# An attention and MLP kernel: key and value tokens laid out four and three to a partition, and a new order of the first batch's steps

## The chip, the core and the metric

The kernel runs on one core of a Trainium2 chip. Its metric is the device time of one execution in microseconds (us). The engines have names of two to four letters: PE multiplies matrices, DVE and ACT work on vectors, POOL is the general engine that also issues the loads which change their type, and SP issues all other loads and stores. Each engine has its own queue of instructions and takes them strictly in order; semaphores tie the queues together. SBUF is the on-chip memory of 128 partitions, PSUM the memory into which PE writes.

## What is computed

Eight batches of twelve heads, 448 tokens of 64 numbers each. Queries and keys are normalized by their root mean square and a gain, then comes softmax attention without a mask. The heads' results, side by side, are the rows of a 3584 x 768 matrix that goes through an MLP with 2048 hidden units and the tanh form of GELU.

```python
q_n, k_n = rmsnorm(q, g_q), rmsnorm(k, g_k)          # x / sqrt(mean(x*x) + 1e-6) * g
scores = scale * q_n @ k_n.T                         # per batch and head, scale = 1/8
attn = exp(scores - max) / sum(exp(scores - max))
x = (attn @ v).transpose(0, 2, 1, 3).reshape(3584, 768)
h = x @ w_in                                         # 768 -> 2048
out = gelu_tanh(h) @ w_out                           # 2048 -> 768
```

The order of a batch's keys within a head is free, as long as keys and values are laid out alike: attention sums over them.

## The kernel before

**Pairs and chunks.** The twelve heads of a batch are six pairs (`hp` 0 to 5), three chunks `c` of two pairs `j` = 0 and 1. For a chunk, `load_q` (L114) and `load_k` (L130) bring queries and keys into the tiles `rawq` and `rawk` (four buffers each). All these loads are issued by SP in the order of `loads` (L146): queries of pair 0, keys of pair 0, queries of pair 1, keys of pair 1, and two small ones.

**Where the keys lie.** 448 keys are three full tiles of 128 and a rest of 64. A key tile has seven slots per chunk (`NS` = 7): slots 0 to 2 hold the first 384 keys of pair 0, slots 4 to 6 those of pair 1, and slot 3 is shared: the last 64 keys of pair 0 lie in partitions 0 to 63, those of pair 1 in 64 to 127 (`own(j)`, L127). `main(j)` loads 384 keys over 128 partitions, three in a row to a partition; `last(j)` loads the other 64. Values follow the same places: `vb` holds three slots of each head, `vr` the rest, with zeros in the partitions of the other pair. `load_v` (L151) is issued by POOL, which turns float32 into bfloat16 on the way: part 0 loads `vb`, parts 1 and 2 load `vr`.

**From raw to exponentials.** Per chunk and pair: squares (`square`, L174), sums of squares on DVE (`total`, L202), one over the root by a logarithm and an exponential on ACT (`rsqrt`, L205), the product with it (`normed`, L219), transposes on PE (`trans`, L231), copies from PSUM into `qT` and `kT` on DVE or ACT (`place_q`, `place_k`). `scores` (L300) then computes one of seven tiles of a chunk ("r" is the shared slot) and returns its exponential, which runs on ACT. Two places in PSUM take scores (`spots`), a third after `third` (L294), and the MLP's first product (`mm1`, L399) uses the same places.

**Sums and products.** `pair_products` (L350) with `what` = 0 sums a pair's exponentials on PE, with `what` = 1 it multiplies them by the values. In the first batch both come in two halves (`sa`, `sb` and `xa`, `xb`). `recip_in`, `recip` and `recip_out` turn the sums into reciprocals on DVE by a transpose, a reciprocal and a transpose back, and `pair_x` multiplies.

**The order of the first batch.** In the first batch the order of all engines' work is written out by hand, in the string `FRONT` (L761), whose steps `front` (L669) issues one by one; each engine gets its instructions in that order. A letter behind the colon says on which engine a step runs (A for ACT, D for DVE, P for POOL). The names:

- `sq`, `sk`: squares of queries or keys of pair i; `tq`, `tk`: their sums; `nq`, `nk`: norms; `tpq`, `tpk`: transposes; `cq`, `ck`: copies out of PSUM
- `rs` i: the roots of pair i; `rS` c: the roots of both pairs of chunk c
- `s` n, `e` n: scores and exponential of tile n, 0 to 20, seven per chunk; `st`, `rc`, `rb`, `xt`: the steps behind a pair's sums
- `v` i, `w` i, `o` i: loads of values, of a quarter of `w_in`, of a quarter of `w_out`, all on POOL; `L` bc: the loads of batch b, chunk c, on SP
- `y` n: n products of zeros on PE, 224 columns each (`idle`, L214), whose result nobody reads
- `gcol`, `shift`: the gains and a bound for the exponent; `mb`, `ma`, `mc`, `md`: parts of the MLP's first product, `g` its GELU; capital letters (`Sq`, `Tk`, `Rs`, `Nk`, `Tp`, `Cq`): the second batch's squares, sums, roots and so on; `V` its values; `GELU`, `EXP`: loads of ACT's function table

**Later batches.** From the second batch on, `attention` (L513) weaves a batch's scores and products with the MLP's second product (`mm2`, L431) of the batch before, so that PE always has something to do; loads come one or two batches ahead, and keys and queries are transposed by DMA (`dma_trans`, L266).

## Time and profile before

| | us |
|---|---|
| median of 3 runs (lowest, highest) | 413.26 (412.65, 413.44) |
| the profiled execution, its own time | 413.83 |
| the profiled execution, its span | 412.1 |

| engine | busy us | share of the span |
|---|---|---|
| PE | 403.7 | 98% |
| ACT | 296.2 | 72% |
| DVE | 274.3 | 67% |
| POOL | 131.8 | 32% |

The span runs from the first to the last instruction of the program. All times inside it count from its start. A row of the list in order of time gives start, duration, engine, line of the kernel, operation, what is written and read, their shapes, and in brackets how long the engine had been idle and what ended that. An engine with a q behind its name (SPq) is its sequencer, which issues DMAs. The granted clock is the share of its full clock at which PE was allowed to run. The trace lacks a few per cent of the products, so counts of them are a little low.

### The profile page before, as it was taken

To read this page: it belongs to the slowest core of one execution; us is meant where nothing else is said; L and a number is where in the kernel's file an instruction comes from. 1 tells how busy PE (TensorE), PEld (TensorE's weight loads), DVE (VectorE), ACT (ScalarE), POOL (GpSimd) and SP (SyncE) were. 2 spreads that over 40 slices of the span, in tenths; PEclk is the share of its full clock that TensorE was granted. 3 is DMA by queue.
4 is the path that set the end of the run, shared out by engine and by line. 5 is a ranking of instruction groups with operands and counts; after the bars stand their busy time and mean duration, and the time that the engine had idled before them with its cause. 6 is when DMAs were issued, how large, how long until landed. Compare 5 with 4: busy or idle time off the path is not lost.

```text
span 412.1 us, 10085 instructions
## 1 busy us (share of the span) xinstructions
PE 403.7 (98%) x4207; PEld 243.5 (59%) x4207; DVE 274.3 (67%) x454; ACT 296.2 (72%) x398; POOL 131.8 (32%) x144
## 2 busy tenths in 40 slices
PE   8799999999999999999999999999999999999996
PEld 3344555566655666557655666556655575556664
DVE  4899739899899638884678747786488633783010
ACT  5797987969988587767977778785976558774300
POOL 7689000234500942037500745019310460000000
PEclk9699999999999999999999999999999999999999
DMA  8999995999981689229981399616991161210022
GB/s 191 227 235 228 203 196 141 227 227 192 213 145 38 139 176 207 66 52 176 222 140 41 78 203 171 136 40 145 171 145 40 23 112 40 72 46 2 2 77 78
DMA packets 97870, 54.21 MB, mean 132 GB/s; under 512 B 63776, under 2 KB 94368, under 8 KB 97824
## 3 DMA queue, kind: packets, MB, share of 16 engines
q1 hardware_dynamic: 71392, 41.69, 43.4%
q0 software_dynamic: 26112, 11.80, 22.5%
q8 instruction: 33, 0.54, 0.6%
q10 hardware_dynamic: 320, 0.07, 0.1%
q14 instruction: 13, 0.11, 0.1%
HBM read 45.61 MB, written 11.01 MB: 137 GB/s over the span
## 4 chain that ended last, share of the span: by engine, by line
PE 95%; SPq 2%; DMA 1%; DVE 0%; ACT 0%; issue 0%; ACTq 0%; DVEq 0%
PE o L441 36%; PE hh L412 31%; PE o L370 11%; PE sc L324 8%; PE h L412 5%; PE sc L310 1%; DMA rawq<-in_q_dram 1%; PE ox L370 1%; SPq L143 1%; SPq L118 1%; SPq L136 1%; PE tp L245 0%; PE o L477 0%; PE tp L238 0%; ACT ex L331 0%
## 5 line engine op out<-in xcount | busy, mean ns | idle before, releaser
L441 PE MATMUL o<-wout,g 128*64 128x384 bf16 (+1 forms) x1648 | 160.6, 327 | 0.0
L331 ACT ACTIVATE ex<-sc,shift 128x896 bf16<-128x896 f32 x144 | 136.1, 1011 | 1.3 <-PE sc L324 1.3
L412 PE MATMUL hh<-xT,win 128*64 128x448 bf16 (+1 forms) x1260 | 133.8, 353 | 0.0
L441 PEld LDWEIGHTS <-g 128*64 128x64 bf16 (+1 forms) x1648 | 96.2, 109 | 58.3 <-issue 14.8
L412 PEld LDWEIGHTS <-win 128*64 128x64 bf16 (+1 forms) x1440 | 95.4, 109 | 49.9 <-issue 3.2
L421 ACT ACTIVATE g<-hh 128x896 bf16<-128x896 f32 x56 | 50.1, 919 | 44.5 <-PE hh L412 44.4
L203 DVE TENSOR_REDUCE ss<-sq 128x14 f32<-128x896 f32 (+4 forms) x45 | 47.9, 1080 | 32.4 <-ACT sq L186 19.9
L454 ACT COPY osb<-o 128x384 f32<-128x384 f32 x50 | 24.2, 483 | 47.8 <-PE o L441 47.8
L788 POOL COPY mark<-es 1x1 bf16<-1x1 bf16 x8 | 1.8, 225 | 162.9 <-DVE es L345 158.5
L377 DVE STREAM_TRANSPOSE st<-o 128x448 f32<-128x448 f32 x48 | 31.1, 648 | 23.6 <-PE o L370 23.2
L324 PE MATMUL sc<-qT,kT 64*128 64x448 bf16 (+1 forms) x372 | 39.6, 360 | 1.7 <-DVE kT L264 1.3
L345 DVE TENSOR_TENSOR es<-ex 128x896 bf16<-128x896 bf16 x42 | 26.8, 637 | 12.0 <-ACT ex L331 12.0
L226 POOL TENSOR_TENSOR nrmq<-rawq,rinv 112x512 bf16<-112x512 f32 x33 | 34.0, 1043 | 0.0
L226 POOL TENSOR_TENSOR nrmk<-rawk,rinv 128x512 bf16<-128x512 f32 (+1 forms) x33 | 31.1, 957 | 4.2 <-ACT rinv L212 4.2
L385 DVE STREAM_TRANSPOSE rb<-rc 128x448 f32<-128x448 f32 x48 | 31.0, 645 | 1.6
L370 PE MATMUL o<-ex,vb 128*64 128x448 bf16 x252 | 30.9, 352 | 0.0
L279 DVE TENSOR_SCALAR kT<-kT,gcol 128x896 bf16<-128x896 bf16 x19 | 21.1, 1108 | 11.7 <-DMA kT<-nrmk 11.7
L343 DVE TENSOR_TENSOR es<-es,exr 64x896 bf16<-64x896 bf16 x42 | 25.9, 617 | 2.4 <-ACT exr L331 1.0
L345 DVE TENSOR_TENSOR es<-es,ex 128x896 bf16<-128x896 bf16 x42 | 25.5, 608 | 2.3 <-ACT ex L331 0.3
L395 DVE TENSOR_TENSOR xT<-o,rb 128x448 bf16<-128x448 f32 x42 | 25.8, 615 | 1.4 <-PE o L370 0.9
L188 POOL TENSOR_TENSOR sq<-rawq 112x1024 f32<-112x1024 f32 x9 | 17.0, 1893 | 28.4 <-DMA rawq<-in_q_dram 25.0
L324 PEld LDWEIGHTS <-kT 64*128 64x128 bf16 (+1 forms) x372 | 10.9, 99 | 24.6 <-issue 18.1
(83 smaller groups left out, 349.4 us busy)
## 6 DMA issues: line engine op xcount, KB each, us to landing
rawq<-in_q_dram SPq DMA_DIRECT2D x48, 224.0 KB, 4.4
rawk<-in_k_dram SPq DMA_DIRECT2D x48, 192.0 KB, 4.6
vb<-in_v_dram POOLq DMA_DIRECT2D x8, 576.0 KB, 10.1
win<-in_moe_w_in_dram POOLq DMA_DIRECT2D x4, 768.0 KB, 14.1
wout<-in_moe_w_out_dram POOLq DMA_DIRECT2D x4, 768.0 KB, 20.4
out_dram<-osb SPq DMA_DIRECT2D x7, 336.0 KB, 4.3
out_dram<-osb SPq DMA_DIRECT2D x8, 288.0 KB, 2.7
out_dram<-osb SPq DMA_DIRECT2D x8, 240.0 KB, 2.6
```

Source lines behind the costliest of these rows:

```text
L203: nc.vector.reduce_sum(stat(ssq[b % 3], b, c, n, j), view(n, sqs[n, b, c], j), axis=AX.X)
L226: eng.tensor_mul(dst.rearrange("p t a d -> p a t d"), view(n, raws[n, b, c], j), r.to_broadcast(list(r.shape) + [D]),)
L324: nc.tensor.matmul(sc[o, a, :S], kT[r, c, 4 * j + t, o], qT[b][r, hp], start=True, stop=True,)
L331: nc.scalar.activation(dst, sc[:, :, :S], AF.Exp, scale=scale, bias=shift)
L343: nc.vector.tensor_add(es[p], es[p], exrs[b, hp // 2][p])
L345: nc.vector.tensor_add(es, ex[:, 0] if t == 1 else es, ex[:, t])
L370: nc.tensor.matmul(o[a * D:(a + 1) * D], w(a), e[:, a], start=(i == 0), stop=(i + 1 == len(steps)),)
L377: nc.vector.transpose(oas["st"].rearrange("p a b -> p (a b)"), oas[0])
L385: nc.vector.transpose(oas["rb", hp], oas["rc"].to_broadcast([128, S // 32, 32]))
L412: nc.tensor.matmul(h[i * m:(i + 1) * m, j, :S], win[:, c // 2 + NCH * (c % 2), f * 128 + i * m:f * 128 + (i + 1) * m], xT[b][:, c], start= ...
L421: nc.scalar.activation(g[:, fs[0]:fs[0] + len(fs), (b % 2) * S:(b % 2 + 1) * S], hs1[fs[0]][:, :, :S], AF.Gelu_apprx_tanh)
L441: nc.tensor.matmul(o[j * m:(j + 1) * m, :HD], g[:, f, i * 128 + j * m:i * 128 + (j + 1) * m], wout[:, f, half * HD:(half + 1) * HD], start ...
```

## The change

Three things change together.

- **Layout of keys and values.** The first 256 keys of a head now lie four in a row in the 64 partitions of `own(j)`, the other 192 three in a row in the other 64 partitions. Both parts of a pair's keys are loads over 64 partitions (`part`), in the order queries, keys, keys per pair. The slots of `rawk` and `kT` are used as before, the shared slot included. Values get a fourth slot in `vb`, and `vr` goes; what was zero in `vr` is zero in `vb`. A batch's values are four loads, two in part 0 and one each in parts 1 and 2.
- **Products with the values.** The same eight products per pair, in the same order; the ones with the shared slot now read `vb`.
- **Order of the first batch.** `FRONT` is a new string: the second chunk's roots are one step (`rS1`), some squares and norms run on another engine, values are loaded in another order, `w0` to `w3` are issued later, zero products stand in other places (`y` 4, 4, 2, 1, 1, 1 instead of 3). The loads of the second batch's first chunk are the first step of `FRONT` instead of standing in front of it. A step `H` is defined, which the string does not use.

```diff
-    vb = [wts.tile([128, H, NK, D], BF16, name=f"vb{i}") for i in range(2)]
-    vr = [wts.tile([128, 2, HP, D], BF16, name=f"vr{i}") for i in range(2)]
+
+    vb = [wts.tile([128, H, NK + 1, D], BF16, name=f"vb{i}") for i in range(2)]
...
-    SM = 128 * NK
+    SM = 64 * (NK + 1)
+
+    def keys(j, n):
+        return (own(j), slice(0, SM)) if n > NK else (own(1 - j), slice(SM, S))
...
-        def main(j):
+        def part(j, n):
+
+            at, span = keys(j, n)
+            s = slice(NK * j + j * (n == NK), NK * j + j * (n == NK) + n)
             h = head(c, j)
             nc.sync.dma_start(
-                t[:, :, 4 * j:4 * j + NK],
-                k[b, h:h + 2, :SM].rearrange("a (p t) d -> p a t d", t=NK),
+                t[at, :, s], k[b, h:h + 2, span].rearrange("a (p t) d -> p a t d", t=n)
             )
-
-        def last(j):
-            h = head(c, j)
-            nc.sync.dma_start(t[own(j), :, NK], k[b, h:h + 2, SM:].rearrange("a p d -> p a d"))
-        return [lambda: main(0), lambda: main(1), lambda: last(0), lambda: last(1)]
+        return [lambda j=j, n=n: part(j, n) for j in range(2) for n in (4, 3)]
 
     def loads(b, c):
         lq, lk = load_q(b, c), load_k(b, c)
-        for go in (lq[0], lk[0], lq[1], *lk[1:]):
+        for go in (lq[0], *lk[:2], lq[1], *lk[2:]):
             go()
 
     def load_v(b, part):
-        if part == 0:
+
+        for j, n in ((0, NK), (1, NK)) if part == 0 else ((part - 1, NK + 1),):
+            at, span = keys(j, n)
+            first = j * (n == NK)
             nc.gpsimd.dma_start(
-                vb[b % 2].rearrange("p h t d -> p h (t d)"),
-                v[b, :, :SM].rearrange("h (p t) d -> p h (t d)", t=NK),
-            )
-        else:
-            j = part - 1
-            nc.gpsimd.dma_start(
-                vr[b % 2][own(j), j], v[b, HP * j:HP * j + HP, SM:].rearrange("h p d -> p h d")
+                vb[b % 2][at, HP * j:HP * j + HP, first:first + n].rearrange("p h t d -> p h (t d)"),
+                v[b, HP * j:HP * j + HP, span].rearrange("h (p t) d -> p h (t d)", t=n),
             )
...
         if what:
-            steps = [(main[t], lambda a, t=t: vb[b % 2][:, head(c, j) + a, t]) for t in range(NK)]
-            steps.append((exrs[b, c], lambda a: vr[b % 2][:, j, 2 * c + a]))
+            steps = [
+                (e, lambda a, t=t: vb[b % 2][:, head(c, j) + a, t])
+                for t, e in enumerate(main[:NK * (1 - j)] + [exrs[b, c]] + main[:NK * j])
+            ]
+            if j:
+                steps.append(steps.pop(0))
...
     loads(0, 2)
-    loads(1, 0)
...
     for i in range(2):
-        nc.gpsimd.memset(vr[i], 0.0)
+        for j in range(2):
+            nc.gpsimd.memset(vb[i][own(1 - j), HP * j:HP * j + HP, NK * (1 - j)], 0.0)
...
     FRONT = """
-        sq0:A sk0:P gcol tq0 tk0 sq1:P rs0 sk1:A nq0:P v1 nk0:D shift tq1 tk1 sq2:A tpq0 tpk0 v2
-        v0 sk2:A rs1 sq3:A cq0:D ck0:D tq2 s0 e0 y3 s1 nk1:D nq1:D L11 e1 tpk1 tpq1 s2 sk3:P w0
-        tq3 tk2 rs2 e2 ck1:D cq1:D s3 e3 sa0 s4 sk4:P tk3 nq2:D nk2:D rs3 tpk2 tpq2 s5 sb0 tk4
-        ck2:D cq2:D nq3:D st0 e4 nk3:P e5 s6 sk5:P L12 e6 tpk3 tpq3 s7 e7 s8 sa1 s9 sb1 xa0 e8
-        sq4:P sq5:P w1 rc0 cq3:D rb0 ck3:D tq4 tk5 rs4 e9 xb0 s10 st1 xt0 rc1 rb1 tq5 e10 sa2
-        s11 e11 rs5 nk4:P nq4:P w2 nk5:P nq5:P xa1 xb1 sb2 s12 e12 s13 tpk4 tpq4 xt1 st2 ck4:D
-        cq4:D rc2 xa2 e13 rb2 sa3 xb2 s14 tpk5 tpq5 s15 e14 xt2 ck5:D cq5:D sb3 e15 U s16 s17
-        xa3 xb3 s18 w3 o0 Sk0:P e16 st3 rc3 rb3 e17 xt3 e18 s19 sa4 xa4 sb4 xb4 Tk0 st4 rc4 s20
-        mb0 mb1 mb2 mb3 sa5 e19 e20 o1 Sq0:P Sq1:P V0 rb4 GELU xt4 Tq0 xa5 sb5 xb5 st5 V1 V2 o2
-        o3 Sk1:A rc5 rb5 ma1 mc0 mc1 xt5 md0 ma2 md1 mc2 md2 Tq1 Tk1 g0 EXP md3 Rs0 g1 Nk00:D
-        Nq11:D Nq00:D Tp0 md4 Cq0:A g2 Sq2:A g3 Nk10:D Nk01:D Nq01:D Ck0:D Tp1 md5 Sk2:A Tq2 Tk2
-        Nk11:D Nq10:D Ck1:A g4 Cq1:A g5 md6 md7 g6 g7 md8 g8
+        L10 sq0:A tq0 sk0:D tk0 gcol rs0 sk1:A sq1:P v1 nq0:P v2 nk0:D tq1 tk1 shift sq2:A rs1
+        tpk0 y4 tpq0 y4 v0 nq1:P sq3:A sk2:P ck0:D cq0:D s0 e0 s1 y2 nk1:D L11 e1 tpk1 s2 tpq1
+        sk3:P e2 ck1:D tq2 cq1:D s3 y1 sa0 s4 e3 s5 sb0 tk2 tq3 tk3 sk4:P rS1 e4 nk2:D nq2:D s6
+        tpk2 y1 tpq2 y1 tk4 st0 ck2:D cq2:D e5 sq4:A nk3:P nq3:P sq5:P w0 sk5:P L12 e6 tpk3 s7
+        sa1 e7 s8 tpq3 sb1 s9 xa0 rc0 tq4 rb0 ck3:D tq5 cq3:D st1 e8 rs4 e9 xb0 s10 xt0 tk5 rc1
+        e10 sa2 s11 xa1 sb2 xb1 s12 rs5 e11 e12 nk4:P nq4:P nq5:P nk5:P w1 w2 w3 Sk0:P rb1 st2
+        xt1 tpq4 tpk4 s13 xa2 e13 cq4:D ck4:D tpq5 s14 tpk5 xb2 s15 sa3 sb3 e14 cq5:D rc2 rb2
+        ck5:D xt2 e15 U s16 s17 s18 xa3 xb3 e16 st3 rc3 rb3 e17 xt3 o0 Sq0:P e18 sa4 s19 sb4 xa4
+        xb4 mb0 mb1 s20 st4 Tk0 rc4 mb2 mb3 Sq1:A e19 e20 rb4 xt4 Tq0 sa5 sb5 xa5 xb5 st5 o1
+        Sk2:P V0 V1 V2 Sk1:A GELU Sq2:A o2 rc5 rb5 mc0 ma1 mc1 xt5 md0 md1 ma2 mc2 md2 Tk1 Tq1
+        g0 EXP Rs0 g1 g2 md3 Nq00:D Nk00:D Tp0 md4 o3 g3 Ck0:A Nk10:D Nk11:D Nq01:D Nq11:D
+        Nk01:D Nq10:D Cq0:D md5 Tp1 g4 g5 Ck1:D Tq2 Cq1:D Tk2 md6 md7 g6 g7 md8 g8
 """
```

More of the change, by code (lines that the diff above doesn't have):

```diff
@@ L112, in head, with raw_q @@
         return 2 * c + HP * j
+    def raw_q(b, c):
+        if ("q", b, c) not in raws:
+            raws["q", b, c] = rawqk.tile([P, CH, NQ, D], F32, tag="rawq", name="rawq")
+        return raws["q", b, c]
     def load_q(b, c):
-        t = rawqk.tile([P, CH, NQ, D], F32, tag="rawq", name="rawq")
-        raws["q", b, c] = t
+        t = raw_q(b, c)
         return [
@@ L734, in front @@
             loads(*divmod(i, 10))
+        elif name == "H":
+            eng.memset(raw_q(*divmod(i, 10))[:1, 0, 0, :1], 0.0)
         elif name in ("Sq", "Sk"):
```

## The prediction

> **What bounds the kernel now.** I read the page first, then busy time by stretch, then the instructions in order of time up to the second batch.
>
> ```profile
> span 412.1 us, 10085 instructions
> PE 95%; SPq 2%; DMA 1%; DVE 0%; ACT 0%; issue 0%; ACTq 0%; DVEq 0%
> ```
>
> TensorE (PE) carries 95% of the chain that ended last, so time can only come from where it idles, repeats work or runs slowly. The second view finds those places. Its columns after the stretch are the length, then busy time and count on PE, weight loads, VectorE (DVE), ScalarE (ACT) and GpSimd (POOL), then the granted TensorE clock, DMA share and GB/s.
>
> ```profile
> 7.17:14.00 6.83, 4.34 (x34) 2.06 (x32) 6.11 (x13) 4.71 (x8) 6.06 (x7) 1.00 1.22 227
> 14.00:20.83 6.83, 6.05 (x37) 2.45 (x36) 5.57 (x13) 5.67 (x9) 4.03 (x5) 0.50 1.37 230
> 20.83:27.66 6.83, 6.42 (x63) 2.96 (x62) 6.72 (x15) 6.51 (x11) 5.45 (x6) 1.00 1.17 243
> 27.66:37.20 9.54, 9.54 (x85) 4.34 (x81) 8.80 (x16) 9.21 (x10) 9.51 (x9) 1.00 1.19 230
> 37.20:54.85 17.65, 17.65 (x105) 9.27 (x104) 11.28 (x17) 13.16 (x18) 3.67 (x5) 1.00 1.37 202
> 54.85:340.00 285.15, 285.15 (x3202) 177.04 (x3203) 208.19 (x330) 219.04 (x293) 98.46 (x101) 1.00 0.69 137
> ```
>
> From 54.85 us to 340 us PE never idles: whatever moves there moves nothing. The tail behind it isn't touched. What this change can win lies before 54.85 us: 2.49 us of idle PE in 7.17 to 14.00, and one stretch of 6.83 us at half clock. The start of the second batch's scores at 54.85 is therefore the mark; if they start x earlier, the kernel ends x earlier.
>
> The third view gives the rows of the first batch that set that mark (start, duration, engine, line).
>
> ```profile
> 11.13 1.91 ACT L331 ACTIVATE ex<-sc,shift 128x896 bf16<-128x896 f32 x2
> 14.39 0.31 ACT L209 ACTIVATE lg<-ss,eps 128x14 f32<-128x14 f32 x1 [1.36 <-DVE ss L203]
> 14.85 0.99 ACT L331 ACTIVATE ex<-sc,shift 128x896 bf16<-128x896 f32 x1
> 17.11 1.01 ACT L331 ACTIVATE ex<-sc,shift 128x896 bf16<-128x896 f32 x1
> 19.77 1.01 ACT L331 ACTIVATE ex<-sc,shift 128x896 bf16<-128x896 f32 x1 [0.37 <-PE sc L324]
> 21.09 1.90 ACT L331 ACTIVATE ex<-sc,shift 128x896 bf16<-128x896 f32 x2 [0.31 <-PE sc L324]
> 25.12 1.00 ACT L331 ACTIVATE ex<-sc,shift 128x896 bf16<-128x896 f32 x1
> 32.25 2.82 ACT L331 ACTIVATE ex<-sc,shift 128x896 bf16<-128x896 f32 x3
> 37.20 5.09 PE L412 MATMUL hh<-xT,win 128*128 128x448 bf16 x26
> 54.85 0.74 PE L324 MATMUL sc<-qT,kT 64*128 64x448 bf16 x6
> ```
>
> The 21 exponentials (e0 to e20) start at 11.13 and end at 32.25 + 2.82 = 35.07, 23.94 us for 21 pieces of some 0.94 (2.82 / 3), so 4.2 us are gaps and roots. The largest gap is the 1.36 us in front of the root at 14.39: it waits on DVE for a sum of squares, and e2 (14.85) is queued behind it on ACT although its scores are ready. After 37.20 PE runs through.
>
> **The change part by part.** All times below are on the clock of this execution.
>
> ```profile
> 1.19 0.46 SPq L136 DMA_DIRECT2D rawk<-in_k_dram  x1
> 2.75 1.41 SPq L143 DMA_DIRECT2D rawk<-in_k_dram  x2
> 6.13 1.04 POOL L188 TENSOR_TENSOR g<-rawq 112x512 f32<-112x512 f32 x1 [0.93 <-DMA rawq<-in_q_dram]
> 7.13 1.36 POOL L226 TENSOR_TENSOR nrmq<-rawq,rinv 112x512 bf16<-112x512 f32 x1
> 8.43 1.48 POOL L159 DMA_DIRECT2D vr<-in_v_dram  x2
> 8.78 1.27 DVE L203 TENSOR_REDUCE ss<-g 112x8 f32<-112x512 f32 x2
> 9.96 0.38 DVE L255 COPY qT<-tp 128x448 bf16<-128x448 bf16 x1
> 10.26 0.41 DVE L264 TENSOR_SCALAR kT<-tp,gcol 128x384 bf16<-128x384 bf16 x1
> 10.54 0.61 ACT L186 ACTIVATE g<-rawq 112x512 f32<-112x512 f32 x1
> 11.02 0.46 PE L217 MATMUL w<-zeros 128*128 128x224 bf16 x3
> 11.71 1.04 POOL L188 TENSOR_TENSOR g<-rawk 128x512 f32<-128x512 f32 x1 [0.76 <-DMA rawk<-in_k_dram]
> 11.78 1.53 DVE L226 TENSOR_TENSOR nrmq<-rawq,rinv 112x512 bf16<-112x512 f32 x1
> 12.71 0.89 POOL L630 DMA_DIRECT2D win<-in_moe_w_in_dram  x1
> 13.62 0.84 POOL L188 TENSOR_TENSOR g<-rawk 128x384 f32<-128x384 f32 x1
> 15.57 0.67 DVE L226 TENSOR_TENSOR nrmq<-rawq,rinv 112x512 bf16<-112x512 f32 x1
> 16.17 0.54 DVE L226 TENSOR_TENSOR nrmk<-rawk,rinv 128x384 bf16<-128x384 f32 x1
> ```
>
> *Loads of keys.* Two issues over 128 partitions (0.46 each) and two over 64 (1.41 / 2 = 0.70) become four over 64. A chunk costs SP 4 x 0.70 instead of 2 x 0.46 + 1.41: 0.47 more. No row shows 64 partitions with runs of 1024 or 768 bytes; its bounds are 0.46 and 0.70, and I take 0.70 as the nearer in partitions. It lies behind the transfers, which are saturated (DMA share 1.22 to 1.37 from 7.17 to 20.83), and the bytes of a chunk stay. With that cover gone the second half of a later chunk lands up to 0.5 later per chunk. In the other batches PE hides it whole. The Trainium skill, "DMA: Bandwidth & Descriptors", Rules for kernel authors, speaks against such a split: two transfers to disjoint partition halves serialize, and one over 128 partitions is to be used. By that rule the split earns nothing and its issue times come out as loss; what that makes here is rival 5.
>
> *Loads of v.* Three issues (two of 0.74, and one over 128 partitions) become four over 64, some 3.0 us of POOL. What counts is place: one issue now stands between POOL's square (6.13 to 7.17) and the norm nq0, which starts at 7.9 instead of 7.13; three more stand ahead of nq1, now on POOL. Queued behind them: nq1, then the squares sk2, sk3 and the root over both.
>
> *First pair.* The square sk0 moves from POOL to DVE; no row shows an f32 product of that form on DVE; its bounds are 0.54 (the norm at 16.17) and 0.84 (POOL at 13.62), I take 0.54. Behind the sum over q it ends no earlier than on POOL: nothing gained. nq0 ends at 7.9 + 1.04 = 8.95 (8.49 before). DVE reaches ck0 and cq0 after two sums (end 8.9) and three small steps of the shift (some 0.5): 9.4 + 0.41 + 0.38 = 10.2. Scores 0.36 later, 10.6; but ACT must first do sq3, whose load doesn't come earlier (it ran at 10.54 before; I take 10.2 + 0.61). So e0 at 10.85: 0.3 gained.
>
> *Roots of the second chunk at once.* e0 to e3 now follow each other: e3 ends at 10.85 + 4 x 0.94 = 14.6. e3 needs nq1: POOL 8.95 + 3 x 0.74 + 1.04 = 12.2, transposes and copy (0.38) and scores: 13.4, just in time. The one root over 30 columns needs both POOL squares: 12.2 + 0.84 + 1.04 = 14.1, a sum 0.64 (1.27 / 2), then 0.46 as between 14.39 and 14.85, and the steps from engine to engine: e4 at 15.35 instead of 17.11. Lead 1.75. One root fewer, 0.46, is in it.
>
> *The lead is spent.* sq4 moves to ACT: 0.61 ahead of e6, which still starts at 17.9 instead of 19.77. For e7, DVE does nk2 and nq2 from 15.35 (0.54 + 0.67) while POOL does nk3 and nq3. At 11.78 such a norm on DVE, beside the POOL square of 11.71, took 1.53 instead of 0.67; the bounds of that penalty are 0 and 0.86, and I take half. With a sum, a transpose and two copies (0.64 + 0.65 + 0.41 + 0.38: DVE done at 19.0) and scores e7 starts at 19.4 instead of 21.09: lead 1.7. Then DVE has reciprocal and transpose of pair 0 (38.64 - 36.93 - 0.65 = 1.06), three sums (1.92), a transpose, a product (0.62) and two copies (0.79), 5.0 together, before the root of the third chunk's second half: 18.7, from overlaps of some 0.06 a step, + 5.0 + 0.46 puts e11 at 24.2 instead of 25.12. From there the exponentials run on: e18 at 24.2 + 7 x 0.94 = 30.8 instead of 32.25. Sq1 of the second batch, now on ACT between e18 and e19, is twice the 0.61 of 10.54 at most; I take 1.1. e20 ends at 34.7: 0.4 gained.
>
> ```profile
> 35.63 1.21 DVE L203 TENSOR_REDUCE ss<-sq 112x16 f32<-112x1024 f32 x1
> 36.93 0.65 DVE L377 STREAM_TRANSPOSE st<-o 128x448 f32<-128x448 f32 x1
> 38.64 0.62 DVE L395 TENSOR_TENSOR xT<-ox,rb 128x448 bf16<-128x448 f32 x1
> 40.12 0.92 ACT L421 ACTIVATE g<-hh 128x896 bf16<-128x896 f32 x1 [2.78 <-PE hh L412]
> 45.25 2.43 PE L412 MATMUL hh<-xT,win 128*128 128x448 bf16 x12
> ```
>
> *The end of the first batch.* Only the last sums wait for e20. PE gets through them at some 36.0 instead of 37.20, and its twelve products before md0 (12 x 5.09 / 26 = 2.35) end at 38.35 instead of 39.55. md0 also needs the last product on DVE (38.64 + 0.62 = 39.26 before). Its chain, 2.33 from the transpose at 36.93 to that end, now stands behind the sum Tq0 (1.21, the form of 35.63): from 34.9 that ends at 36.1, and 36.1 + 2.33 = 38.4. So md0 at 38.5 to 38.6 instead of 39.55. The first gelu (40.12) follows it, then two table loads with the root between, the second gelu, and the products at 45.25 that wait for its place: 0.9 to 1.0 earlier, as the two sums that this root still needs (2 x 1.21) end on DVE at 40.8. The squares of the second batch that change engines lie behind PE's products.
>
> *Zero products.* Three go, thirteen come, each 0.46 / 3 = 0.15 alone: 1.5 us of PE, where it otherwise waits for norms; without that wait they would cost it.
>
> *Weights.* w0's issue moves from 12.71 behind the square sq5 (15.35 + 3 x 1.04 and half the penalty) to 19, and its products start behind e18. The view of this tile gives
>
> ```profile
> DMA to landing us min/median/max: 11.6/14.1/15.7
> ```
>
> from issue to landing, for parts that all had v or another part ahead on their queue; w0 now has nothing ahead. Bounds: 19 + 11.6 to 19 + 15.7, or earlier by the wait it no longer has. I take 29 and no cost; at 34.7 it would hold PE's first eight products by 2 us, which the last key sums could partly fill. The zeroing of v's unused places is as large as before, and POOL waits for data then.
>
> *Sum.* 0.3 at e0, 1.7 at e7, 0.4 at e20, but 0.9 at md0, since PE and DVE had less left behind the exponentials. So -0.9 +- 0.5 at 54.85, and at the end. This execution took 413.83 by its own time (span 412.1, 1.7 around it): 412.9. The median of three is 413.26, 0.57 less: **412.35**.
>
> **The clock.** This sum holds at full clock. The stretch from 7.17, PE busy 4.34 of 6.83 (64%), is followed by half clock; those with 6.05 (89%) and 6.42 (94%) by full. So the limit of what counts as busy lies between 64% and 89%. Changed, the first gains eight zero products net, a score and the first key sums, 1.2 to 2.2 us: 81 to 95%, probably enough. The next stretch, now at full speed, does the same work in less time; I put it at 65 to 85%. The Trainium skill, "TensorE: Matmul & The Clock Gate", Why this matters for your kernels, asks only that no gap exceeds about 3 us. By that rule neither kernel would lose its clock, and rivals 1 and 2 would have no chance; the trace disagrees: the stretch before the slow one has only 2.49 us of idle time in all.
>
> **The rivals.**
> 1. *The slow stretch moves to 20.83 to 27.66.* For: the 65 to 85% above. Against: it is only about half of the open interval. Price: before has 63 products there, 0.098 each (half of 5.09 / 26, as most use half of the array) and the transposes among them half of that, 4.5 to 5.5 us with what has been done earlier; at half clock 9 to 11, 2.2 to 4 more than the 6.83 hold. Less the lead of 0.9: +1.3 to +3; I take the lower end, as PE also has short waits there to fill, +1.2: 414.45, slower. It decides from the point where the loss exceeds 0.9.
> 2. *It stays at 14.00 to 20.83.* Transposes and scores on e7's path take 0.2 each longer, and the sums too: 0.5 lost, 412.85. For: ten small zero products are little work. Against: the 81 to 95%.
> 3. *The lead is eaten.* DVE and POOL get in each other's way at nk2/nq2 beside nk3/nq3 by the full 0.85, nq1 comes late for e3, and Sq1 (1.06) stands in front of e19: e20 no earlier, 413.3. For: the row at 11.78. Against: DVE and PE have less left behind e20.
> 4. *The lead lasts*, should the third chunk's root not hold e11: 1.7 as at e7, 411.55. Against: DVE is busy for 6.72 of 6.83 us from 20.83.
> 5. *The split loads cost their issue.* The queries of the second chunk come behind one chunk's 0.47 more on SP, sq3 and e0 with them: 412.35 + 0.5 = 412.85. Against: the DMA share above 1.2 says that data, not issue, is late.
>
> **How the numbers follow.** Forecast 0.52, rivals 0.18, 0.12, 0.10, 0.04 and 0.04. Beyond 0.2% (0.83 us, about what a measurement of this kernel tells from no change) lie 412.43 and 414.09. Faster: 0.36 of the forecast (its centre is just past the bound, and between bounds I mostly took the longer step), 0.02 of rivals 2 and 5, 0.04 of rival 4: 0.42. Slower: 0.16 of rival 1, 0.02 of rival 3, 0.01 of the forecast: 0.19. Same: 0.39. The range for 8 in 10 is 411.4 to 414.5: the top reaches rival 1's price, the bottom rival 4's. The forecast's own range is 411.85 to 412.85.
>
> **What would show it.** Right: e2 directly behind e1, one root before e4 at 15 to 15.6, e7 near 19.4, e20 ending near 34.7, md0 near 38.5, second batch's scores near 53.9, full clock throughout. Wrong: half clock at 14.00 or 20.83; a norm on POOL or DVE over 1.3 us; e3 waiting for nq1; any PE idle after the second batch's scores.

## The result and the profile after

| | before | after |
|---|---|---|
| median, us | 413.24 | 414.19 |
| lowest to highest of 22 runs | 412.11 to 414.29 | 413.36 to 416.59 |
| ratio after / before, 95% interval | | 1.0033 (1.002 to 1.0045) |
| profiled execution, its own time | 413.83 | 414.39 |
| its span | 412.1 | 412.6 |

The change makes the kernel 0.95 us slower; the forecast was 0.9 us faster. First the view of busy time by stretch, in the stretches and columns of the prediction, and the one row for all that follows the mark.

```profile
7.17:14.00 6.83, 5.21 (x42) 2.53 (x41) 6.27 (x14) 5.24 (x9) 6.81 (x9) 1.00 1.11 211
14.00:20.83 6.83, 4.50 (x34) 1.90 (x33) 5.47 (x12) 5.29 (x8) 4.88 (x6) 0.87 1.24 212
20.83:27.66 6.83, 6.83 (x59) 2.71 (x57) 5.40 (x12) 6.15 (x11) 5.30 (x6) 0.88 1.18 219
```

```profile
55.43:340.00 284.57, 284.57 (x3198) 177.00 (x3199) 209.15 (x330) 218.56 (x292) 101.13 (x107) 1.00 0.68 139
```

In 7.17 to 14.00 PE is busier (5.21 for 4.34), as forecast. In 14.00 to 20.83 it is busy for 4.50 where before had 6.05: new waits, though part of those 6.05 us is products that ran at half clock. A clock of 0.87 and 0.88 in two stretches is one piece of half clock that lies across 20.83. The same view in stretches of 3.41 us places it:

```profile
12.29:15.70 3.41, 2.83 (x23) 1.00 (x21) 2.89 (x6) 2.95 (x5) 2.11 (x3) 1.00 1.24 202
15.70:19.11 3.41, 1.25 (x15) 0.81 (x12) 2.56 (x6) 3.31 (x5) 2.77 (x3) 1.00 1.28 220
19.11:22.53 3.42, 3.36 (x20) 1.21 (x19) 2.88 (x8) 1.87 (x2) 3.40 (x4) 0.50 1.13 223
22.53:25.94 3.41, 3.41 (x34) 1.41 (x32) 2.52 (x6) 3.10 (x8) 1.90 (x4) 1.00 1.21 206
```

PE is busy for 1.25 of 3.41 us from 15.70, and half clock follows, 19.11 to 22.53. From there on PE has no idle time: what it loses at half clock in that stretch is not made up in this execution. What made the stretch from 15.70 so empty is in the list in order of time:

```profile
10.98 2.80 ACT L334 ACTIVATE ex<-sc,shift 128x896 bf16<-128x896 f32 x3
15.57 0.23 ACT L215 ACTIVATE rinv<-lg 128x30 f32<-128x30 f32 x1
15.70 1.89 ACT L334 ACTIVATE ex<-sc,shift 128x896 bf16<-128x896 f32 x2
16.34 1.33 POOL L191 TENSOR_TENSOR g<-rawk 128x384 f32<-128x384 f32 x1 [1.95 <-DMA rawk<-in_k_dram]
16.74 0.36 PE L327 MATMUL sc<-qT,kT 64*128 64x448 bf16 x2 [0.85 <-ACT ex L334]
17.63 1.04 POOL L229 TENSOR_TENSOR nrmk<-rawk,rinv 128x512 bf16<-128x512 f32 x1
17.70 0.55 DVE L206 TENSOR_REDUCE ss<-g 128x6 f32<-128x384 f32 x1 [0.72 <-POOL g L191]
18.74 0.38 DVE L267 TENSOR_SCALAR kT<-tp,gcol 128x384 bf16<-128x384 bf16 x1
19.17 0.59 PE L248 MATMUL tp<-ident,nrmk 128*128 128x128 bf16 x4 [1.38 <-DVE kT L267]
20.28 1.01 ACT L334 ACTIVATE ex<-sc,shift 128x896 bf16<-128x896 f32 x1 [1.28 <-PE sc L327]
```

```profile
34.49 1.95 ACT L334 ACTIVATE ex<-sc,shift 128x896 bf16<-128x896 f32 x2
37.83 7.75 PE L419 MATMUL hh<-xT,win 128*128 128x448 bf16 x40
55.43 0.74 PE L327 MATMUL sc<-qT,kT 64*128 64x448 bf16 x6
```

Exponentials e0 to e2 follow each other from 10.98, as forecast, and e4 starts at 15.70 (forecast 15.35). Then POOL's square at 16.34 (`sk4`, the first keys of the third chunk) has waited 1.95 us for its load; DVE's sum at 17.70 waits for the square; behind it in DVE's queue are the transpose `st0` and the copy `ck2` (18.74), for which PE waits 1.38 us. An earlier wait of 0.85, at 16.74, is for e4 (15.70), which stands behind the root at 15.57. e7 starts at 20.28 (forecast 19.4). e20 ends at 34.49 + 1.95 = 36.44 (forecast 34.7) and the mark, the second batch's scores, stands at 55.43: 0.58 later than 54.85, and the span is 0.5 longer.

The chain of waits in order of time (start, duration, what) says the same from the other end:

```profile
0.74 0.39 SPq L122
1.19 0.75 SPq L146
...
9.07 0.60 SPq L146
9.71 6.57 DMA rawk<-in_k_dram
16.34 1.34 POOL g L191
17.70 0.55 DVE ss L206
18.26 0.56 DVE st L384
18.82 0.31 DVE kT L267
19.17 0.59 PE tp L248 x4
```

What sets the time PE starts its last unbroken run in this execution is SP: fifteen issues one behind the other from 0.74, the last at 9.71, then 6.57 us until that load has landed at 16.28. In before the same square ran at 13.62 without a wait (its row is in the prediction).

### The profile page after: what moved, and what is told of

Its sections match the earlier page's. It is cut to its first block, busy times and chain, and to the rows that moved or that the text cites. A ratio compares the mean times of both kernels' runs of the same rounds, so it can differ in the third digit from the quotient of the medians.

```text
span 412.6 us, 10137 instructions
## 1 busy us (share of the span) xinstructions
PE 404.0 (98%) x4217; PEld 243.3 (59%) x4217; DVE 274.7 (67%) x455; ACT 295.7 (72%) x394; POOL 135.7 (33%) x155
## 4 chain that ended last, share of the span: by engine, by line
PE 94%; SPq 2%; DMA 2%; DVE 0%; POOL 0%; issue 0%; ACTq 0%; ACT 0%; DVEq 0%
PE o L448 36%; PE hh L419 31%; PE o L377 11%; PE sc L327 8%; PE h L419 5%; DMA rawk<-in_k_dram 2%; SPq L146 1%; PE ox L377 1%; PE sc L313 1%; SPq L122 1%; PE o L484 0%; PE tp L241 0%; PE tp L248 0%; POOL g L191 0%; PE o L241 0%
## 5 line engine op out<-in xcount | busy, mean ns | idle before, releaser
L229 POOL TENSOR_TENSOR nrmq<-rawq,rinv 112x512 bf16<-112x512 f32 x35 | 35.8, 1036 | 0.9 <-ACT rinv L215 0.9
L377 PEld LDWEIGHTS <-vb 128*64 128x64 bf16 x384 | 21.6, 110 | 12.9 <-issue 0.8
L348 DVE TENSOR_TENSOR es<-es,ex 128x896 bf16<-128x896 bf16 x42 | 26.9, 639 | 2.3 <-ACT ex L334 0.3
```

The lines of the kernel that those rows point to most:

```text
L229: eng.tensor_mul(dst.rearrange("p t a d -> p a t d"), view(n, raws[n, b, c], j), r.to_broadcast(list(r.shape) + [D]),)
L348: nc.vector.tensor_add(es, ex[:, 0] if t == 1 else es, ex[:, t])
L377: nc.tensor.matmul(o[a * D:(a + 1) * D], w(a), e[:, a], start=(i == 0), stop=(i + 1 == len(steps)),)
```

## The experiments

Each ran beside the kernel before on the same chip. The chip differs between groups of runs, and the median of before with it (413.11 to 413.33), so groups are compared by their ratios. The table puts the nineteen profiled fronts (an execution up to the mark) side by side: start of the first exponential, e4 and e7 counted from it, the time at half clock in the front, the mark, PE's waits behind it, and the median of the runs (ratio to before with its interval where there were several rounds).

| kernel | e0 | e4 - e0 | e7 - e0 | half clock | mark | waits behind | median | ratio (95%) |
|---|---|---|---|---|---|---|---|---|
| before | 11.13 | 5.98 | 9.96 | 14.00-20.83 | 54.85 | none | 413.24 | |
| before_again | 10.79 | 4.73 | 9.37 | 10.74-20.98 | 53.92 | 0.23 | 413.31, one run | |
| before_late | 10.44 | 5.13 | 9.19 | 12.61-19.44 | 53.39 | none | 412.82 | 0.9989 (0.9977-1.0) |
| before_fixed | 11.27 | 4.70 | 8.58 | 12.56-19.39 | 54.13 | none | 413.19 | 1.0001 (0.9991-1.0012) |
| before_filled | 10.95 | 4.83 | 7.70 | none | 53.34 | none | 412.79 | 0.9996 (0.9982-1.001) |
| after | 10.98 | 4.72 | 9.30 | 19.11-22.53 | 55.43 | none | 414.19 | 1.0033 (1.002-1.0045) |
| after_again | 11.50 | 4.54 | 8.76 | none | 54.42 | 0.41 | 413.99, one run | |
| after_late | 11.36 | 4.42 | 8.98 | 19.32-22.73 | 55.55 | none | 414.59 | 1.0036 (1.0021-1.005) |
| after_bare | 11.07 | 4.42 | 9.00 | 12.54-22.77 | 55.40 | 0.15 | 414.75 | 1.0048 (1.0029-1.0066) |
| after_filled | 10.98 | 4.52 | 8.93 | none | 55.03 | 0.26 | 413.56 | 1.001 (0.9998-1.0021) |
| after_fixed | 11.57 | 4.31 | 8.50 | none | 54.23 | none | 413.52 | 1.0019 (1.0003-1.0035) |
| sk4_behind | 11.23 | 4.53 | 8.29 | none | 54.46 | 0.74 | 414.91 | 1.0049 (1.0029-1.0068) |
| sk4_late | 11.07 | 4.96 | 9.12 | 17.37-24.19 | 56.11 | none | 414.19 | 1.0025 (1.0013-1.0037) |
| sk4_filled | 11.25 | 4.43 | 8.44 | none | 54.38 | 0.81 | 414.63 | 1.0033 (1.0019-1.0048) |
| order_alone | 11.30 | 4.44 | 8.67 | 19.99-23.40 | 55.55 | 0.70 | 415.65 | 1.0058 (1.0043-1.0073) |
| order_fixed | 10.61 | 4.57 | 8.80 | none | 53.58 | none | 413.38 | 1.0009 (0.9994-1.0023) |
| loads_alone | 11.43 | 4.61 | 8.63 | 13.01-19.84 | 54.02 | 0.81 | 414.03 | 1.0027 (1.0016-1.0038) |
| loads_late | 11.22 | 4.75 | 9.59 | 13.41-23.65 | 55.44 | none | 414.45 | 1.0022 (1.0006-1.0038) |
| v_behind | 11.13 | 4.30 | 8.94 | 19.95-23.37 | 58.35 | none | 417.13 | 1.0095 (1.0082-1.0108) |

A profile shows one execution, the median many; e0 alone moves between 10.4 and 11.6 us. So the profiles are read for mechanisms, the medians for prices.

**Four that part loads from order.** order_alone has the new `FRONT` in the kernel before; loads_alone the old `FRONT` in the changed kernel. The other two edit the new `FRONT`:

```diff
 v_behind
-sq1:P v1 nq0:P v2 nk0:D ... tpq0 y4 v0 nq1:P ... sk4:P rS1 e4
+sq1:P v1 nq0:P nk0:D ... tpq0 y4 nq1:P ... sk4:P v2 v0 rS1 e4
 sk4_behind
-tk3 sk4:P rS1 e4 ... tk4 st0 ck2:D cq2:D e5 sq4:A nk3:P nq3:P sq5:P
+tk3 rS1 e4 ... st0 ck2:D cq2:D e5 sq4:A nk3:P nq3:P sk4:P tk4 sq5:P
```

> The order of the changed kernel with the loads of the kernel before (three issues for v, two of a chunk's four key loads over all 128 partitions). Theory A (the third chunk's first keys land late, at 16.28 us instead of 13.05; GpSimd's square sk4 waits for them, VectorE's sum behind it holds the copies, and e7 starts at 20.28): they land near 14, sk4 starts by 14.6, e7 starts at 19.2 to 19.6 and the second batch's scores at 53.9 to 54.5: 0.4 to 0.9 us faster than before. Rival B (the order itself costs, VectorE and GpSimd hinder each other): e7 stays at 20.1 or later, 0.5 to 1 us slower than before. Rival C (the half clock alone costs it): e7 early, but half the clock somewhere behind 19 us and no gain.

> The loads of the changed kernel (keys and v split in 64 partitions) with the order of the kernel before. Theory A: the third chunk's first keys land some 1.5 us later than in before (13.05), as SP issues them later and they need two loads, so that GpSimd's square sk4 (13.62 before) starts near 14.7; before has slack behind it, so 0 to 0.5 us slower. Rival D (the split itself is the whole loss): 1 us slower or more. Rival B: as before within 0.2 us.

> The changed kernel with three of v's four loads issued behind the square sk4 instead of around nq0 and nq1. Theory A, with v's bytes as the main cause of the delay: the third chunk's first keys land near 15 instead of 16.28, sk4 starts there, e7 at 19.4 to 19.8, the second batch's scores at 54.4 to 54.9: 0.5 to 1 us faster than the changed kernel. If the later and split issue on SP is the main cause: landing after 15.8, 0 to 0.3 us faster. Rival B or C: no gain, or slower because v comes late for its products.

> The changed kernel with the square sk4 on GpSimd behind nk3 and nq3, and its sum on VectorE behind the copies ck2 and cq2: the late keys hold nothing any more. Theory A: nk3 starts at 15.8 instead of 17.63, ck2 at 17.4 to 18.0 instead of 18.74, e7 at 19.2 instead of 20.28; 0.5 to 1 us faster than the changed kernel at the second batch's scores, unless the third chunk's roots then come late (e9 to e11), which would leave e11 near 25.7 and no gain. Rival B: nk2 and nq2 on VectorE beside nk3 and nq3 on GpSimd stretch each other by up to 0.85 and e7 stays at 20 or later. Rival C: e7 early, half the clock stays, gain below 0.3.

All four were slower than before. POOL's rows (order of time) of order_alone and then of loads_alone:

```profile
12.58 2.76 POOL L188 TENSOR_TENSOR g<-rawk 128x384 f32<-128x384 f32 x3
15.91 1.42 POOL L226 TENSOR_TENSOR nrmk<-rawk,rinv 128x512 bf16<-128x512 f32 x1 [0.57 <-ACT rinv L212]
17.29 1.49 POOL L226 TENSOR_TENSOR nrmq<-rawq,rinv 112x512 bf16<-112x512 f32 x1
```

```profile
16.02 0.82 POOL L191 TENSOR_TENSOR g<-rawk 128x384 f32<-128x384 f32 x1 [2.04 <-DMA rawk<-in_k_dram]
```

With the old loads, `sk4` is the third of the squares that run from 12.58 to 15.34 without a wait; with the new loads it waits for its keys until 16.02 even in the old order. So the split loads delay these keys in the old order too: 16.02 against 13.53 to 14.64 in the five profiles of that order with the old loads (theory A's first link). But order_alone shows what comes when the keys are there: the norms nk3 and nq3 on POOL run beside DVE's nk2 and nq2 and take 1.42 and 1.49 instead of 1.04, and e7 comes 8.67 behind e0 (9.30 in after, 8.58 to 9.96 in before's order with its own loads and zero products). In after the wait for keys had kept these norms apart. So theory A alone doesn't hold: order_alone was to be 0.4 to 0.9 faster than before and is 2.3 slower. Its profile shows a mark 0.7 later and a wait of 0.70 behind it; the rest of the 2.3 stays open. In v_behind (only v1 ahead) sk4 starts at 15.44, where unedited after had 16.34 and, profiled again, 15.32; but v then comes late:

```profile
24.45 0.76 PE L377 MATMUL ox<-ex,vb 128*64 128x448 bf16 x6 [1.18 <-DMA vb<-in_v_dram]
...
28.14 0.38 PE L377 MATMUL ox<-ex,vb 128*64 128x448 bf16 x2 [1.32 <-DMA vb<-in_v_dram]
```

These two waits, 2.50 together, are most of the 2.9 us by which it is slower than after; v can't go there. sk4_behind has the earliest e7 of the four (8.29 behind e0), full clock in its profile and a mark of 54.46, yet a median of 414.91. Its runs at full clock took 413.77 to 414.40, the five with a clock of 0.991 or 0.992 took 415.17 to 417.16: the clock decides more than e7 does.

**A wait near 300 us.** loads_alone has its mark 0.83 us earlier than before and still ends no earlier. Its list in order of time:

```profile
296.99 2.99 POOL L191 TENSOR_TENSOR sq<-rawk 128x896 f32<-128x896 f32 x1 [0.34 <-DMA rawk<-in_k_dram]
302.21 1.09 DVE L206 TENSOR_REDUCE ss<-sq 128x14 f32<-128x896 f32 x1
303.21 0.64 DVE L384 STREAM_TRANSPOSE st<-o 128x448 f32<-128x448 f32 x1
303.90 0.76 PE L377 MATMUL o<-ex,vb 128*64 128x448 bf16 x6 [0.81 <-DVE st L384]
```

POOL's square of the last keys runs beside DVE's sums and takes 2.99 (1.68 in before, at 296.65); DVE's sum over it comes at 302.21 instead of 301.43, the transpose behind it at 303.21, and PE waits 0.81 for its place. Four kernels move that sum behind the transpose:

```diff
-((1 + (b == 2)) * (n == "k"), lambda n=n: total(b + 2, 2, n))
+((1 + (b in (2, 5))) * (n == "k"), lambda n=n: total(b + 2, 2, n))
```

> The kernel before, with VectorE's sum over the last key square of the last batch moved from ahead of a pair's transpose (301.43 us, the transpose at 302.79 has 0.27 us to spare) to behind it. Theory L (a stage near 300 us has so little to spare that a square on GpSimd that lands beside VectorE's sums holds the transpose, and PE for 0.7 to 0.8 us): 0 to 0.3 us faster than before, since its profile shows no wait there. Rival (that wait is no cause but follows from something else): no change.

> The changed kernel with the same one move of a sum near 300 us. Theory L: executions at full clock lose 0.8 us there and get it back: median 0.3 to 0.8 us below the changed kernel's 414.19. Theory A alone (all the loss is in the first batch): no change, as the profiled execution of the changed kernel has no wait at 303 us.

> Changed loads, the order of the kernel before, and the sum near 300 us moved. Theory L: the second batch's scores stay at 54.0, the wait of 0.81 us at 303.09 is gone, and the run ends 0.8 us below the 414.03 of the changed loads alone: 413.2, as fast as before. Rival (the changed loads cost in every batch): PE waits elsewhere behind 100 us and 413.8 or more stays.

> The changed kernel with the square sk4 behind nk3 and nq3 and the sum near 300 us moved. Theory A and L together: second batch's scores at 54.0 to 54.6, no wait at 303 us, 413.2 to 413.6 in executions at full clock (0.8 below the 413.8 to 414.4 without the moved sum); executions with a stretch of half clock stay 1 to 3 us above that.

In none of the four profiles does PE wait there (the first profiles of before and after have no such wait either), and the medians don't follow: before_late gains 0.5 at the edge of its interval, which before_fixed (below) doesn't repeat, after_late and loads_late gain nothing, sk4_late 0.7 with intervals that overlap. The wait is real in single executions of both kernels (0.23 in before_again, 0.41 in after_again) but the difference stays where the sum is moved; theory L is not confirmed as a price. Single executions do pay for such waits: from the mark to the end, the eleven profiles without one take 357.2 to 357.4, the eight with one 357.5 to 358.4. What else differs stands in the table. From e0 to the mark, pairs of profiles with the same front took 42.6 and 44.2 (loads_alone, loads_late), 43.2 and 45.0 (sk4_behind, sk4_late), 42.9 and 44.4 (after_again, after): the second of each had half clock in the time behind 19 us, the first none there or 0.84 us of it.

**The clock.** Zero products, whose result nobody reads, are put where PE waits, or taken away; all four keep the moved sum.

```diff
 after_filled:  ... sb0 +y6 tk2 ...  L12 e6 +y10 tpk3 s7 ...
 sk4_filled:    ... sb0 +y6 tk2 ...  L12 e6 +y6 tpk3 s7 ...
 before_filled: ... tq2 +y8 s0 e0 y3 ...  tpk1 +y7 tpq1 ...  cq1:D +y4 s3 e3 ...
 after_bare:    tpk0 -y4 tpq0 -y4 ... e0 +y3 s1 -y2 ... s3 -y1 ... tpk2 -y1 tpq2 -y1
```

> The changed kernel with the moved sum near 300 us, and sixteen more zero products (128x224) on TensorE where it waits: six ahead of the score that waits at 15.9 us for 0.85, ten ahead of the transposes that wait at 17.8 us for 1.38. Theory C (half the clock follows a stretch of 3.41 us in which PE is busy for 0.62 or less; in the changed kernel that stretch is 15.70 to 19.11, busy 0.37, and the half clock falls on 19.11 to 22.53, where PE has no waits left and loses up to 1.7 us): full clock throughout, the second batch's scores at 54.3 to 54.6 instead of 55.5, median 413.4 to 413.7 instead of 414.59. Rival (the clock only follows the late e7, whose price is all): no gain, scores at 55.3 or later; the products may even hold a score by 0.1 to 0.3.

> The changed kernel with the square sk4 behind nk3 and nq3, the sum near 300 us moved, and twelve zero products in the waits at 15.8 and 18 us. Theory A and C together: full clock, e7 at 19.5, second batch's scores at 53.9 to 54.4, median 413.0 to 413.4. Rival B (nk3 and nq3 on GpSimd, 1.4 to 1.5 us each beside VectorE's norms, hold e7 anyway): not better than the filled kernel without the moved square.

> The kernel before with the sum near 300 us moved and nineteen zero products in its three waits (eight ahead of the first score, seven ahead of the second transposes of queries, four ahead of the score at 14 us). Theory C: the stretch of 3.41 us before the slow one, busy 0.62, comes to 0.8 or more; full clock from 14 to 20.8; the gaps of 0.3 to 0.4 us ahead of e4 to e7, where ACT waits for PE's slow products, shrink: 0.3 to 1 us faster than the 412.82 with the moved sum alone. Rival (the slow stretch lies where PE waits anyway and costs nothing): 412.8 again; or the slow stretch moves to 20.8 and costs: 413.5.

> The changed kernel with the moved sum near 300 us and without its thirteen added zero products (the three of the kernel before instead). Theory C: the first stretches are busy 0.55 or less, half the clock falls early (12 to 19 us), where PE waits for others anyway; full clock again from 19 to 21. Second batch's scores at 55.0 to 55.6, median 414.0 to 414.6, no worse than with the zero products although more time runs at half clock. Rival (each us at half clock costs the same, wherever it falls): 1 us slower, 415.5.

Busy time by stretch of 3.41 us: after_filled, before_filled, and after_bare.

```profile
15.13:18.54 3.41, 3.23 (x33) 2.28 (x31) 1.97 (x4) 3.38 (x6) 1.67 (x2) 1.00 1.31 232
18.54:21.95 3.41, 2.99 (x29) 1.27 (x28) 3.41 (x10) 2.31 (x4) 3.39 (x5) 1.00 1.16 189
```

```profile
11.22:14.64 3.42, 3.28 (x33) 1.91 (x31) 3.42 (x8) 3.15 (x6) 2.48 (x3) 1.00 1.36 203
14.64:18.05 3.41, 2.40 (x27) 1.20 (x25) 3.41 (x7) 3.29 (x6) 1.85 (x3) 1.00 1.48 217
```

```profile
9.12:12.54 3.42, 2.10 (x20) 1.09 (x19) 2.89 (x7) 2.40 (x5) 3.42 (x5) 1.00 1.12 213
12.54:15.95 3.41, 3.29 (x18) 1.08 (x18) 2.63 (x6) 3.24 (x6) 1.40 (x2) 0.50 1.31 227
15.95:19.36 3.41, 2.35 (x17) 1.19 (x13) 2.69 (x8) 2.85 (x4) 3.09 (x3) 0.50 1.18 239
19.36:22.77 3.41, 3.41 (x20) 0.96 (x18) 2.43 (x5) 2.30 (x4) 3.00 (x4) 0.50 1.12 228
```

In after_filled the stretch that was busy for 1.25 is busy for 3.23, the clock stays at 1.00, and the median falls from 414.59 to 413.56: 1.0 us, or 0.8 when each is counted from the before beside it (1.26 and 0.45 above), from work that computes nothing. e7 is where it was (8.98 and 8.93 behind e0), so the late e7 is not what costs it. The profiled execution of after_filled (414.49) is one of its slowest and shows no gain; the reading rests on the medians. In before_filled the clock is full as well, and nothing is gained (412.79, with the half clock 412.82): before's half clock has waits of PE behind it (busy for 6.42 of 6.83 us from 20.83), in which lost time can be made up. That this is why it costs nothing is argued, not shown. e7 comes 7.70 behind e0 there, the earliest of all, but PE then waits 0.73 for v:

```profile
21.30 0.76 PE L370 MATMUL ox<-ex,vb 128*64 128x448 bf16 x6 [0.73 <-DMA vb<-in_v_dram]
```

after_bare (its four rows above) is at half clock for 10.2 us instead of 3.4 and is as fast as after_late within the intervals, which fits that most of the added time lies before 19 us. By these medians the price hangs on where the half clock falls: none measured up to some 19 us, 0.8 to 1.0 us where PE has no wait left.

after_filled's first batch then met something new. ACT's rows, then PE's:

```profile
39.34 1.06 ACT L189 ACTIVATE sq<-rawq 112x1024 f32<-112x1024 f32 x1 [1.98 <-DMA rawq<-in_q_dram]
40.31 0.90 ACT L428 ACTIVATE g<-hh 128x896 bf16<-128x896 f32 x1
```

```profile
45.43 1.86 PE L419 MATMUL hh<-xT,win 128*128 128x448 bf16 x9 [0.69 <-ACT g L428]
```

The second batch's square Sq2, which the change put ahead of the first GELU on ACT, waits 1.98 us for its load; GELU, table loads and root follow late, and PE waits 0.69 for a gelu at 45.43. sk4_filled, at full clock and with its square moved, was no better (414.63): a wait of 0.81 at 255.91, one batch ahead of the moved sum, stands in its profile. Why it is 1.1 us above after_filled at the same clock stays open.

**Loads or order, at full clock.** after_fixed and order_fixed move Sq2 back behind the third GELU, keep added zero products (six and ten, six and six) and move the sum in two batches; order_fixed has the loads of before. before_fixed only moves the sums.

```diff
-Sk1:A GELU Sq2:A o2 ... g0 EXP Rs0 g1 g2 md3
+Sk1:A GELU o2 ... g0 EXP Rs0 g1 g2 Sq2:A md3
-(b in (2, 5))
+(b in (2, 4, 5))
```

> The filled changed kernel (sixteen zero products in its waits, key sums of later batches moved near 256 and 303 us) with the second batch's square Sq2 back behind the third gelu, as in the kernel before. Theory D (Sq2 ahead of the first gelu waits 2 us for its load and holds gelu, table loads and root, so that PE waits 0.69 at 44.74): that wait is gone, second batch's scores at 54.2 to 54.5, no wait behind them, median 412.8 to 413.2 instead of 413.56. Rival (the sums over the second batch's keys hold that root anyway): the wait stays, 413.5.

> The changed order with the loads of the kernel before, twelve zero products in its two waits, Sq2 back behind the third gelu, key sums of later batches moved. If the changed loads keep the gain (theory A): e7 at 19.3 to 19.8, e11 at 24.5, second batch's scores at 53.4 to 53.9, median 412.2 to 412.7, below before_fixed. If the order itself does (rival B, norms on GpSimd of 1.4 to 1.5 us beside VectorE's): e7 at 19.9 or later, scores at 54.2 or later, 412.9 to 413.4, not below before_fixed.

> The kernel before with the sums over the last key squares moved behind a pair's transpose in two later batches (near 256 and 303 us). Theory L: 412.7 to 412.9, 0.3 to 0.5 us faster than before. Rival: as before, 413.2.

The wait at 44.74 is gone in after_fixed's profile and its mark is 54.23, as expected, but the median stays at 413.52, so removing that one profile's wait is worth nothing measurable. With the old loads (order_fixed) the profile has e7 at 19.41 and the mark at 53.58, as theory A expected, yet the median is 413.38, with an interval that holds both "as before" and after_fixed: at full clock no gain of the order over before is measured, with either loads. before_fixed is as fast as before.

**Both kernels profiled again, unedited.** The forecast's lead rested on one wait of 1.36 us in one profile.

> The kernel before, unedited, profiled a second time. If the wait of 1.36 us ahead of the root at 14.39 was an accident of the first profile (GpSimd's square there began 0.07 us ahead of VectorE's norm, which then took 1.53 instead of 0.68): the norm takes 0.7, the root waits 0 to 0.6 and e2 starts 1.5 to 2.0 us behind e1 (2.81 in the first profile). If it belongs to the kernel: 2.5 us or more again.

> The changed kernel, unedited, profiled a second time. Theory A and C: third chunk's first keys after 15.9 us, e7 8.3 to 9.4 us behind e0, PE busy for less than 0.62 of some stretch of 3.41 us between 12 and 20 us and half the clock behind it, or, if the grid of stretches falls otherwise, full clock and the second batch's scores 43.0 to 43.5 us behind e0 instead of 44.4.

The rows of before_again, in order of time:

```profile
10.79 1.89 ACT L331 ACTIVATE ex<-sc,shift 128x896 bf16<-128x896 f32 x2
11.03 0.68 DVE L226 TENSOR_TENSOR nrmq<-rawq,rinv 112x512 bf16<-112x512 f32 x1
12.16 1.03 POOL L188 TENSOR_TENSOR g<-rawk 128x512 f32<-128x512 f32 x1 [1.21 <-DMA rawk<-in_k_dram]
12.81 0.31 ACT L209 ACTIVATE lg<-ss,eps 128x14 f32<-128x14 f32 x1
13.27 0.99 ACT L331 ACTIVATE ex<-sc,shift 128x896 bf16<-128x896 f32 x1
```

The norm on DVE starts ahead of POOL's square and takes 0.68 (1.53 in the first profile, where the square at 11.71 was 0.07 ahead of it). The root at 12.81 waits for nothing and e2 starts 1.59 behind e1 (2.81 there). before_fixed (1.56) and before_late (1.97), whose fronts are the same, agree. after_again had full clock, and its mark lies 42.9 behind e0; the forecast had 43.1 (53.95 less 10.85). Its keys came before 15.9 us, against what was expected:

```profile
15.32 0.83 POOL L191 TENSOR_TENSOR g<-rawk 128x384 f32<-128x384 f32 x1 [0.58 <-DMA rawk<-in_k_dram]
```

The long wait of the first profile, 1.95, is thus not in every execution. The norms nk3 and nq3 then took 1.41 and 1.49, and e7 came 8.76 behind e0. Although its mark is 0.4 ahead of that in the first profile of before, its span, 412.2, is no shorter: it has the wait of 0.41 at 303 us.

## Why the prediction was wrong

- **What bounds the kernel.** Right in the main: behind the mark PE's rest is the same in before and after. Not always, though: eight of the other seventeen profiles have a wait of 0.15 to 0.81 near 256 or 303 us, so that "whatever moves there moves nothing" held for the profiled execution and not for all.
- **First pair.** e0 at 10.98 and 11.50 in two profiles (forecast 10.85, before 11.13 and 10.79): no gain beyond the scatter.
- **Roots of the second chunk at once.** The mechanism came as forecast: e2 directly behind e1, one root, e4 at 15.70. The size was wrong. "Lead 1.75" was taken against e4 at 17.11, 5.98 behind e0, an execution in which DVE's norm and POOL's square had collided. In the other profiles of that front e4 comes 4.70 to 5.13 behind e0, and 4.54 to 4.72 in the two of the changed kernel: a lead of 0 to 0.6. The row had said so itself, 1.53 beside 0.67 for the same norm, and the prediction used it only as a price of collisions to come.
- **From own time to median.** The sum subtracted 0.57 for a slow execution and also counted the gain of removing its slow spot. Those are in the main the same time: from e0 to the mark the profiled before took 43.7, before_again 43.1, before_late and before_fixed 42.9.
- **Loads of keys.** "Up to 0.5 later per chunk" and hidden behind saturated transfers: mis-sized. The third chunk's first keys let their square start at 16.34 instead of 13.62, as both halves of the split load are needed and the second is issued at 9.71; whether v's parts, moving at the same time, add to it v_behind doesn't settle. Rival 5 named this cost (0.04) but put it on e0; it fell on sk4. The Trainium skill, "DMA: Bandwidth & Descriptors", Rules for kernel authors, warns of loads split over partition halves, as the two transfers serialize. The trace agrees in the issues, which follow one another on SP (9.07 and 9.71 for the two halves), and in that after's chain of waits runs over them and then over the second load; whether the transfers themselves serialize no run here shows.
- **The lead is spent.** e7 was forecast at 19.4 and came at 20.28, for a reason that the sum didn't have: it counted DVE's sum over sk4 but not the square itself, which stands ahead of nk3 on POOL, waits for its load, and then took 1.33 (0.84 in before) beside DVE's norm at 16.30. Where the keys are there in time (order_alone, after_again), the collision of norms of rival 3 takes the place of the wait.
- **Zero products and weights.** As forecast: no cost of their own (after_bare against after_late), and no wait for w0.
- **Second batch's squares.** "Behind PE's products" failed for Sq2 in after_filled (0.69), but only once the front was earlier.
- **The clock.** This is the step behind most of the measured loss. "Full clock throughout" was the forecast, and the doubt about the next stretch (65 to 85%) went into rival 1 with 0.18. PE was busy for 4.50 of 6.83 (66%) there, but for 1.25 of 3.41 in the worst half, because of the two late waits above, and the clock changes by stretches of 3.41; half clock followed at 19.11, and taking it away gave 0.8 to 1.0 us back. That is rival 1, at 414.45, in mechanism and nearly in price, 1.7 us earlier and for half as long. Six of after's 22 runs had full clock; they took 413.36 to 414.22, with a median of 413.87, the median of the others is 414.45. Among the kernel's own runs the clock is thus worth 0.6 us, and at full clock it is still 0.6 above before.

So, of the 1.8 us between forecast and result, 0.6 to 1.0 is the clock (shown by after's own runs, a pair of medians and three pairs of fronts), 0.6 to 0.9 is a lead that before already had in the other three profiles of its front. What is left, up to 0.6 us, stays open. The late waits near 256 and 303 us and Sq2 appear in single profiles; what they cost on the median isn't settled, nor is what remains at full clock (ratios 1.001 and 1.0019, the first with an interval that holds no difference). No version measured beats before beyond its interval.

## What to carry to other kernels

Before a lead is counted from one wait in one profile, ask whether that wait is the kernel's or that execution's: an instruction that took twice its usual time in front of it, and a profiled time above the median, suggest that it is the execution's. Half clock had no price of its own here (412.82 with it, 412.79 without, in before); it cost where the engine had no wait left, so a change that fills early waits and opens later ones can lose more by the clock than it wins by the order. When loads are split, count every issue on the queue, and look for the first instruction that needs both halves.

## What the hardware showed unexpectedly

- The clock changes in steps of 3.41 us, on a grid that starts at 3.8 to 7.2 us in the profiles of these fronts, so the same waits may or may not make one stretch empty. In these traces, half clock followed every stretch in which PE was busy for 57% or less (seven of seven, 35 to 57%); 59 to 63% went both ways; none followed 65% or more. It ended only after a stretch of 97% or more; 92 and 96% prolonged it. The Trainium skill, "TensorE: Matmul & The Clock Gate", Why this matters for your kernels, asks for gaps under about 3 us; the longest wait ahead of after's half clock was 1.38 us, so by that rule it would have kept its clock.
- Where products of two f32 tensors on DVE and POOL overlap in these fronts, the one that starts later is as a rule the one that takes longer: DVE's norm 0.68 to 1.53, POOL's norms 1.04 to 1.42 and 1.49. There is an exception: in before_again a norm of DVE at 13.97 started 0.08 ahead of POOL's square, and it was the norm that took longer, 1.49. POOL's square of 896 columns went from 1.68 to 2.99 beside DVE's bf16 sums, and one of these from 0.63 to 1.91.
